# Sums of weights for block products: VectorE additions, or ScalarE copies with accumulating GpSimd transfers

## The chip, the core and the metric

The kernel runs on one core of one Trainium2 chip. A core has five engines that each work through their own queue in order: TensorE (PE in the profile, with its weight loads as PEld), VectorE (DVE), ScalarE (ACT), GpSimd (POOL) and SyncE (SP). SP only issues transfers here; the transfers of all queues run on 16 DMA engines. The metric is the device time of one execution in microseconds.

## The reference

Two parts follow one another. The first is an attention with a decaying state, for 4 batches, 8 heads, 768 tokens and 48 channels per head:

```python
for t in range(S):
    cur = einsum('bhd,bhe->bhde', u * k_t, v_t)
    y[:, :, t] = einsum('bhd,bhde->bhe', r_t, state + cur)
    state = w_t[..., None] * state + einsum('bhd,bhe->bhde', k_t, v_t)
```

Its output, laid out as 3072 tokens by 384 channels, is the input `x` of the second part. Its weights are `w_in` (384 by 2048) and `w_out` (2048 by 384), given in 64-bit floating point:

```python
h = x @ w_in
g = h * clip(h + 3.0, 0.0, 6.0) / 6.0
out = g @ w_out
```

## The kernel before

**Tiling.** The tokens are cut into 24 chunks of 128, and four chunks form a block; there are six blocks. Attention runs chunk by chunk: two scans over the decay on DVE (`back_scan` L372, `fore_scan` L381), products that make K (`make_k` L392) and R (`make_r` L396), score products on PE (L440), a masked copy of them on DVE (`above` L447), a transposition of K (L456) whose result ACT copies (`turned_k`, "kn", L461), diagonal terms on ACT (`diagonal` L431), products that read the state (L514) and the values (L523), products that write the state (`write` L536), and state updates on DVE or POOL (L469, L477, L485). For the first seven chunks `early(i)` puts K and R on DVE, from chunk 7 on it puts them on POOL. `own_dot` (L415) multiplies r, u and k on PE for the first nine chunks. In block 0, `read_last`, `leave_last` (L576), `read_rest` (L584) and `leave_rest` (L594, L596) bring a chunk's output into the block's `xT`.

**The weights** come as 64-bit words in 16 loads of 768 KB into the tile `bits` (three buffers). ACT (`low_scaled` L340, `low_whole` L344) and DVE (`high_shift` L349, `high_join` L354, `high_low` L359) turn each load into 32-bit numbers, by way of the tiles `more` and `top`.

**The products.** Block 0 computes its up products plainly (`up` L639, with `ramp` L629 on ACT and `gate` L650 on DVE behind each), and so its down products for chunks 0 and 1 (`down` L658, `drain` L665). All else is done in 2 by 2 blocks with seven products instead of eight (`up_product` L740, `down_product` L791). This form needs sums of quarters of the operands. The sums of activations are made for every block (`sum_x` L722, `sum_g` L776). The sums of weights are made once, when the last weight is converted: `sum_in` (L700) makes three sums of quarters of `w_in` in the freed buffers `top` and `more` and overwrites one quarter in place, in 16 additions of 128x256. `sum_out` (L712) makes three sums of quarters of `w_out` in the freed `bits` and overwrites one quarter in place, in eight additions of 128x768. The products read the sums; `up_read` (L749 on ACT, L751 on DVE) and `down_read` (L804 on ACT, L806 on DVE) join the seven results.

**The order.** A class `Plan` sets each engine's order. Every step is added with its engine, an assumed duration, the steps it needs, a key, and the rings of buffers it holds. `order()` places the steps one by one: on the engine that can start first, the ready step with the smallest key. Keys are due times, shifted by constants at the top of the file (`LAG`, `AHEAD`, `LEAD`, `START`, `CONV`, `UP`, `SUMS`, `OWN`). The instructions are then issued in that order, and each engine runs its own in order. In the opening, up to the first `up`, `emit` also fills gaps that the plan sees on PE with `spin` matmuls of the identity (L1130), whose results nobody reads:

```python
if engine == "PE" and spinning:
    for _ in range(int(self.FILL * (self.start[n] - last) / self.SPIN)):
        self.spin()
```

The functions that the change touches, and what calls them:

Of the kernel before, what the change touches and what calls it, by code (L numbers as in the profile page):

```python
# [8 lines left out]
F32 = mybir.dt.float32  # L9
# [17 lines left out]

LAG = 6.1
AHEAD = -3.5
LEAD = 2.5  # L30
BEHIND = (-1, -1, -1, 0, 6, 7)
BY_PE = 9
OWN = 0.07
SOLO = (0, 2, 3, 4, 5)
EARLY = 7
START = (-118.3, -135.2, -24.4, -60.3, -5.9, 13.2)
CONV = (-100.6, 7.2)
UP = (-68.7, 1.2, -9.3, 6.3)
SUMS = (52.1, 1.4)
LEAST = 2.0 ** -60  # L40
# [42 lines left out]
class Plan:  # L83
# [20 lines left out]
    def add(self, name, engine, us, emit, after=(), key=0.0, hold=(), port=False, kb=0.0, lands=0.0,  # L104
            dmas=1):

        assert name not in self.steps, name
        self.steps[name] = (engine, us, emit, tuple(after), key, tuple(hold), port, kb, lands, dmas)

    def order(self):  # L110
# [13 lines left out]
        while open_:  # L124
            best = {}
            for n in open_:
                engine, us, _, after, key, hold, shared, kb, _, dmas = steps[n]
                t = free.get(engine, 0.0)
                if kb and len(lanes) + dmas > self.LANES:
                    t = max(t, lanes[len(lanes) + dmas - self.LANES - 1])  # L130
                for a in after:
                    if steps[a][0] != engine:
                        t = max(t, end[a] + self.HOP)
                for r, _ in hold:
                    over = len(held[r]) - self.rings[r]
                    if over >= 0:
                        ends = sorted(max(end[a] + (self.HOP if steps[a][0] != engine else 0.0) for a in frees)
                                      for frees in held[r] if all(a in end for a in frees))
                        if len(ends) <= over:
                            t = None  # L140
                            break
                        t = max(t, ends[over])
                if t is None:
                    continue
                if shared:
                    t = max(t, port)
                best.setdefault(engine, []).append((t, key, n))
            assert best, sorted(open_)
            t, engine = min((min(c)[0], e) for e, c in best.items())
            _, _, n = min((key, t_, n) for t_, key, n in best[engine] if t_ <= t + 1e-9)  # L150
            _, us, _, _, _, hold, shared, kb, lands, dmas = steps[n]
            start[n] = t
            free[engine] = end[n] = t + us
            if kb:
# [3 lines left out]
                end[n] = max(done + self.LAND, lands)  # L158
                lanes += [end[n]] * dmas
            if shared:  # L160
                port = t + us
# [26 lines left out]
def fast_path(tc, feat, tok, wflat, ub, ug, moe_w_in, moe_w_out, out, flag, n_chunks):  # L188
# [21 lines left out]
    with ExitStack() as ctx:  # L210
# [475 lines left out]

        def sum_in(s, q):

            at = (s - 1 if s < 3 else 2) * HF + q
            if s != 3 and at // 6 not in a_sums:  # L690
                name = ("top", "more")[at // 6 % 2]
                a_sums[at // 6] = wk.tile([128, 6 * 128], F32, name=name)
            (a11, a21), (a12, a22) = ([w_in[:, q:q + 2, j, y, :] for y in range(2)] for j in range(2))
            def sums(k):
                at = k * HF + q
                return a_sums[at // 6][:, at % 6 * 128:(at % 6 + 2) * 128].rearrange("p (q j) -> p q j", q=2)
            out_, in0, in1, op = {1: lambda: (sums(0), a21, a22, ALU.add), 2: lambda: (sums(1), sums(0), a11, ALU.subtract),
                                  3: lambda: (a21, a11, a21, ALU.subtract),
                                  4: lambda: (sums(2), a12, sums(1), ALU.subtract)}[s]()
            nc.vector.tensor_tensor(out=out_, in0=in0, in1=in1, op=op)  # L700

        def sum_out(t, x):

            m, h = HF // 2, DM // 2
            if t != 3 and x == 0:
                b_sums[t] = io.tile([128, HF, h], F32, name="bits", bufs=3)
            (b11, b12), (b21, b22) = ([w_out[:, k * HF + x * m:k * HF + (x + 1) * m, y * h:(y + 1) * h] for y in range(2)]
                                      for k in range(2))
            T = {k: v[:, x * m:(x + 1) * m, :] for k, v in b_sums.items()}
            out_, in0, in1 = {1: lambda: (T[1], b12, b11), 2: lambda: (T[2], b22, T[1]), 3: lambda: (b12, b22, b12),  # L710
                              4: lambda: (T[4], b21, T[2])}[t]()
            nc.vector.tensor_tensor(out=out_, in0=in0, in1=in1, op=ALU.subtract)  # L712

        def sum_x(bk, part):
# [4 lines left out]
            (b11, b12), (b21, b22), (c1, c2) = ([b["xT"][:, j, y * HB:(y + 1) * HB] for y in range(2)] for j in range(NCC))  # L719
            for o, x, y in (((T[:, 0], b12, b11), (T[:, 1], b22, T[:, 0])),  # L720
                            ((b12, b22, b12), (T[:, 2], b21, T[:, 1]), (T[:, 3], c1, c2)))[part]:
                nc.vector.tensor_tensor(out=o, in0=x, in1=y, op=ALU.subtract)  # L722

# [19 lines left out]
        def up_read(bk, q, what):  # L743
# [3 lines left out]
            src = b["p", q, {"s1": "A", "u": "A", "c21": "A", "c22": "A", "c11": "B", "v": "C", "c12": "C"}[what]][:, :HB]  # L747
            if what in ("s1", "u", "v", "c21"):
                nc.scalar.copy(out=to, in_=src)  # L749
            else:  # L750
                nc.vector.tensor_add(to, src, to)  # L751

# [8 lines left out]
        def sum_g(bk, p, k, x):  # L761
# [7 lines left out]
            def part(h, c):  # L769
                if bk == 0:  # L770
                    return b["g", h][:, x * m:(x + 1) * m, (2 * p + c) * L:(2 * p + c + 1) * L]
                return b["g", p][:, h * HF + x * m:h * HF + (x + 1) * m, c * L:(c + 1) * L]
            (a11, a21), (a12, a22) = ([part(h, c) for c in range(2)] for h in range(2))
            o, x0, x1, op = {1: (S, a21, a22, ALU.add), 2: (S, S, a11, ALU.subtract), 3: (a21, a11, a21, ALU.subtract),
                             4: (S, a12, S, ALU.subtract)}[k]
            nc.vector.tensor_tensor(out=o, in0=x0, in1=x1, op=op)  # L776
# [17 lines left out]
        def down_read(bk, p, what):  # L794
            b = blocks[bk]
            h = DM // 2
            if what == "s1":
# [3 lines left out]
                  "v": o[:, 1, h:], "c22": o[:, 1, h:]}[what]  # L801
            src = b["d", p, {"s1": "A", "u": "A", "c21": "A", "c22": "A", "c11": "B", "v": "C", "c12": "C"}[what]][:, :h]
            if what in ("s1", "u", "v", "c21"):
                nc.scalar.mul(to, src, 1.0 / 6.0)  # L804
            else:
                nc.vector.scalar_tensor_tensor(out=to, in0=src, scalar=1.0 / 6.0, in1=to, op0=ALU.mult, op1=ALU.add)  # L806

# [59 lines left out]
        def do(fn, *args):  # L867
            return lambda: fn(*args)
# [154 lines left out]

        for n_, (s_, q) in enumerate((s_, q) for s_ in (1, 2, 4, 3) for q in range(0, HF, 2)):
            at = ({1: 0, 2: 1, 4: 2}.get(s_, 9)) * HF + q
            hold = []
            if s_ != 3 and at % 6 == 0:
                hold = [(("top", "more")[at // 6 % 2], ["end"])]
            before = [f"sin{x}.{q}" for x in ({2: (1,), 4: (2,)}.get(s_, ()))] + [f"sin{s_}.{q - 2}"] * (q > 0)
            if s_ == 3:  # L1030
                before += all_up + [f"sin1.{q}"]
            if s_ == 1 and q == 0:
                before += [f"{ready}{len(pairs) - 1}"]
            if s_ in (2, 4) and q == 0:
                before += [f"sin{s_ // 2}.{HF - 2}"]
            plan.add(f"sin{s_}.{q}", "DVE", 0.36, do(sum_in, s_, q), before, SUMS[0] + n_ * SUMS[1] / 4, hold, port=True)
        for n_, (t_, x) in enumerate((t_, x) for t_ in (1, 2, 4, 3) for x in range(2)):
            before = [f"sout{y}.{x}" for y in ({2: (1,), 4: (2,)}.get(t_, ()))] + [f"sout{t_}.0"] * x
            if t_ == 3:
                before += [f"down0.{c}.{HF - 1}" for c in classic] + [f"sout1.{x}"]  # L1040
            if t_ == 1 and x == 0:
                before += [f"{ready}{len(pairs) - 1}"]
            plan.add(f"sout{t_}.{x}", "DVE", 0.95, do(sum_out, t_, x), before, SUMS[0] + 4 * SUMS[1] + n_ * SUMS[1] / 2,
                     [("bits", ["end"])] * (t_ != 3 and x == 0), port=True)
        sin = [f"sin{s_}.{HF - 2}" for s_ in range(1, 5)]
        sout = [f"sout{t_}.1" for t_ in range(1, 5)]

        for bk in range(NB):
# [34 lines left out]
            for p in range(bk == 0, 2):  # L1083
# [14 lines left out]
                for n_, (k_, after, hold) in enumerate((  # L1098
                        (1, [], [("bankA", [r + "c21"])]), (2, [], [("bankB", [r + "c11"])]), (5, [], [("bankC", [r + "c12"])]),
                        (6, [r + "s1"], []), (3, [r + "v"], []), (7, [r + "u"], []), (4, [r + "c22"], []))):  # L1100
                    for x in range(2):
                        before = gated(0, NFC) if k_ != 1 else gated(4 * x, 4 * x + 4)
                        if k_ in (5, 6, 7, 3):
                            before = [g_ + f"{ {5: 1, 6: 2, 7: 3, 3: 4}[k_] }.{x}"]
                        chain = {6: 1, 7: 6, 4: 7, 3: 5}.get(k_)
                        plan.add(d_ + f"{k_}.{x}", "PE", 1.3, do(down_product, bk, p, k_, x),
                                 before + [d_ + f"{k_}.0"] * x + [d_ + f"{chain}.1"] * bool(chain) + after + [f"sout{t_}.{x}" for t_ in ({5: 1, 6: 2, 7: 3, 4: 4}.get(k_),) if t_], at + 2.6 * n_ + 1.3 * x + (2.6 if k_ == 4 else 0), hold if x == 0 else ())
                for what, eng, after, key in (("s1", "ACT", [d_ + "1.1"], 1), ("v", "ACT", [d_ + "5.1"], 3), ("u", "ACT", [d_ + "6.1"], 4),
# [361 lines left out]
```

## Time and profile before

| | value |
|---|---|
| median of 3 runs (lowest to highest) | 573.67 us (573.64 to 573.75) |
| span of the profiled execution, first to last instruction | 570.5 us |
| its own time beside the span | not recorded apart; the median of the runs lies 3.2 us above the span |
| mean granted TensorE clock | 0.992 |
| busy: PE, PEld, DVE, ACT, POOL | 558.8, 501.8, 405.2, 273.5, 100.3 us |
| DVE sums of weights, 16 of L700 and 8 of L712 | 7.5 and 8.5 us, between 102 and 133 us |
| first product of `up` | 32.3 us |

Times in the profile count from the first instruction. A matmul of 32-bit numbers shows as two records. PE's busy time is modelled from its queue, so a busy PE isn't PE at its peak, and filler counts as busy. Granted clock is the share of full speed that the array was given. A wait is put down to the engine that came last.

### The profile page before, as it was taken

How to read it: one execution, taken by the hardware profiler on the slowest of the kernel's cores; microseconds unless marked ns; L12 is line 12 of the kernel's file. 1: busy time of each engine (PE TensorE's matmuls, PEld its weight loads, DVE VectorE, ACT ScalarE, POOL GpSimd, SP SyncE). 2: the span in 40 equal slices, each digit the busy share in tenths (PEclk: the TensorE clock that was granted, in tenths of full speed). 3: DMA queues.
4: the chain of work that ended last, by engine and by line, in shares of the span. 5: the costliest groups of instructions: out<-in, count | busy, mean ns of one | idle time of the engine just before them, and what ended most of it. 6: DMA issues, size and time to landing. Idle time of an engine off the chain costs nothing.

```text
span 570.5 us, 13575 instructions
## 1 busy us (share of the span) xinstructions
PE 558.8 (98%) x5636; PEld 501.8 (88%) x5636; DVE 405.2 (71%) x713; ACT 273.5 (48%) x724; POOL 100.3 (18%) x111
## 2 busy tenths in 40 slices
PE   8999899999999999999999999999999999999996
PEld 8898587689888999988999988999988999988996
DVE  7989989988687858767879767879656625255350
ACT  4778664642565633276633366633266611355100
POOL 2000000245513321223123133123122000000000
PEclk9989899999999999999999999999999999999999
DMA  8977822531613236830368360366100001000001
GB/s 279 310 237 223 275 66 63 158 111 42 182 56 90 87 124 204 241 100 9 125 206 274 98 167 7 128 199 225 41 16 2 9 1 36 29 1 1 1 15 47
DMA packets 23078, 63.98 MB, mean 112 GB/s; under 512 B 3120, under 2 KB 10352, under 8 KB 23008
## 3 DMA queue, kind: packets, MB, share of 16 engines
q1 hardware_dynamic: 22880, 63.02, 36.0%
q8 instruction: 46, 0.75, 0.6%
q14 instruction: 24, 0.20, 0.1%
q10 hardware_dynamic: 128, 0.00, 0.0%
HBM read 57.31 MB, written 4.72 MB: 109 GB/s over the span
## 4 chain that ended last, share of the span: by engine, by line
PE 94%; DVE 2%; DMA 1%; ACT 1%; issue 1%; SPq 0%; DVEq 0%; ACTq 0%
PE bankA L791 20%; PE bankA L740 18%; PE bankC L791 10%; PE bankC L740 9%; PE bankB L740 6%; PE bankB L791 5%; PE bankC L639 3%; PE bankA L639 3%; PE bankA L658 3%; PE y_ps L514 3%; PE y_ps L523 2%; PE y_ps L536 2%; PE ps L456 2%; PE bankB L440 2%; DMA feat_in<-in_feat_dram 1%; PE bankA L1130 1%
## 5 line engine op out<-in xcount | busy, mean ns | idle before, releaser
L749 ACT COPY g<-bankA 128x256 f32<-128x256 f32 x120 | 44.3, 371 | 58.7 <-PE bankA L740 56.6
L791 PE MATMUL bankA<-w_out,g 128*128 128x192 f32 x352 | 63.9, 328 | 0.0
L629 ACT ACTIVATE clip<-g,three 128x512 f32<-128x512 f32 x80 | 57.9, 723 | 7.9 <-DVE g L751 7.2
L740 PE MATMUL bankA<-xT,w_in 128*128 128x256 f32 x240 | 60.2, 383 | 0.0
L791 PEld LDWEIGHTS bankA<-w_out,g 128*128 128x128 f32 x352 | 57.9, 190 | 0.9
L759 DVE SCALAR_TENSOR_TENSOR g<-clip,g 128x512 f32<-128x512 f32 x80 | 56.4, 707 | 2.8 <-ACT clip L629 2.6
L804 ACT ACTIVATE o<-bankA 128x192 f32<-128x192 f32 x33 | 10.9, 330 | 88.8 <-PE bankA L791 88.8
L740 PEld LDWEIGHTS bankA<-xT,w_in 128*128 128x128 f32 x240 | 44.8, 190 | 6.0
L431 ACT ACTIVATE A<-eyes,dg 128x64 f32<-128x64 f32 x192 | 49.2, 336 | 0.4
L606 ACT COPY xT<-y_ps 48x256 f32<-48x256 f32 x80 | 29.3, 366 | 37.3 <-PE y_ps L523 36.4
L392 POOL TENSOR_TENSOR K<-feat_in,E 112x512 f32<-112x512 f32 x17 | 21.5, 1266 | 136.6 <-PE bankC L440 121.6
L740 PE MATMUL bankB<-xT,w_in 128*128 128x256 f32 x160 | 41.1, 379 | 0.0
L751 DVE TENSOR_TENSOR g<-bankB,g 128x256 f32<-128x256 f32 x40 | 16.9, 423 | 32.4 <-PE bankB L740 30.7
L396 POOL TENSOR_TENSOR W<-feat_in,W 112x512 f32<-112x512 f32 x17 | 23.1, 1356 | 87.2 <-DVE W L381 87.2
L751 DVE TENSOR_TENSOR g<-bankC,g 128x256 f32<-128x256 f32 x40 | 16.8, 421 | 28.3 <-PE bankC L740 28.2
L740 PEld LDWEIGHTS bankB<-xT,w_in 128*128 128x128 f32 x160 | 30.4, 190 | 4.1
L381 DVE TENSOR_TENSOR_SCAN W<-feat_in,start 112x520 f32<-112x520 f32 x24 | 30.6, 1274 | 3.1 <-PE y_ps L514 3.0
L372 DVE TENSOR_TENSOR_SCAN E<-feat_in,back 112x520 f32<-112x520 f32 x24 | 30.0, 1250 | 2.5 <-DMA feat_in<-in_feat_dram 2.4
L791 PE MATMUL bankA<-bits,g 128*128 128x192 f32 x176 | 30.3, 328 | 0.4 <-DVE o L806 0.4
L791 PE MATMUL bankB<-w_out,g 128*128 128x192 f32 x176 | 30.4, 326 | 0.0
L791 PEld LDWEIGHTS bankA<-bits,g 128*128 128x128 f32 x176 | 28.8, 190 | 0.9 <-DVE o L806 0.7
L791 PEld LDWEIGHTS bankB<-w_out,g 128*128 128x128 f32 x176 | 28.9, 190 | 0.0
(277 smaller groups left out, 1213.8 us busy)
## 6 DMA issues: line engine op xcount, KB each, us to landing
feat_in<-in_feat_dram SPq DMA_DIRECT2D x23, 675.9 KB, 5.6
bits<-in_moe_w_in_dram SPq DMA_DIRECT2D x8, 768.0 KB, 9.6
bits<-in_moe_w_out_dram SPq DMA_DIRECT2D x8, 768.0 KB, 4.7
feat_in<-in_moe_w_in_dram SPq DMA_DIRECT2D x8, 768.0 KB, 4.3
feat_in<-in_moe_w_out_dram SPq DMA_DIRECT2D x8, 768.0 KB, 4.2
rk_in<-in_tok_dram SPq DMA_DIRECT2D x15, 384.0 KB, 5.9
v_in<-in_tok_dram SPq DMA_DIRECT2D x24, 192.0 KB, 4.0
out_dram<-o SPq DMA_DIRECT2D x24, 192.0 KB, 2.1
```

The lines of the kernel that those rows point to most:

```text
L372: nc.vector.tensor_tensor_scan(out=E_[:, ::-1], data0=d["w"][:, :0:-1], data1=back.rearrange("q p t -> q (p t)")[:, ::-1], initial=0.0, op ...
L381: nc.vector.tensor_tensor_scan(out=W_, data0=d["w"][:, :-1], data1=starts[i % 2].rearrange("q p t -> q (p t)"), initial=0.0, op0=ALU.mult, ...
L396: early(i).tensor_mul(d["R"], d["r"], d["R"])
L431: nc.scalar.activation(out=d["A"][:, h, :], in_=eyes, func=ACT.Copy, scale=d["dg"][:, h])
L606: nc.scalar.copy(out=blocks[bk]["xT"][g * GP:g * GP + D, :, at:at + HL], in_=st[i]["y_ps"][(g ^ a) * GP:(g ^ a) * GP + D, a, :, :])
L629: nc.scalar.activation(out=c[:, :m], in_=src, func=ACT.Relu, bias=three, scale=1.0)
L639: nc.tensor.matmul(h_ps[:, :(c1 - c0) * L], lhsT=w_in[:, f // 2, j, f % 2, :], rhs=b["xT"][:, j, c0 * L:c1 * L], start=(j == 0), stop=(j = ...
L740: nc.tensor.matmul(b["p", q, to][:, :HB], lhsT=w, rhs=rhs, start=(n == 0 and k in (1, 2, 5)), stop=(n == len(terms) - 1 and k in (2, 3, 4) ...
L749: nc.scalar.copy(out=to, in_=src)
L751: nc.vector.tensor_add(to, src, to)
L759: nc.vector.scalar_tensor_tensor(out=g, in0=b["r", q, p], scalar=6.0, in1=g, op0=ALU.min, op1=ALU.mult)
L791: nc.tensor.matmul(b["d", p, to][:, :h], lhsT=a, rhs=w(), start=(f == 0 and k in (1, 2, 5)), stop=(f == HF - 1 and k in (2, 3, 4)), skip_g ...
```

## The change

The sums of weights leave VectorE. For each sum ScalarE first copies one quarter into the new tile (`begin_out`, `begin_in`), and then a transfer issued by GpSimd adds the other quarter to it on the way (`accum_op=ALU.add`). The second sum of a chain adds the first, the third adds the second, so each of these transfers waits until the one before has landed. The two quarters that are overwritten get their addition by a transfer alone. There are 13 transfers: four for `w_out`, nine for `w_in`, because tiles of `top` and `more` hold six of eight pieces.

A transfer can add[...], so signs move: ScalarE negates one quarter of `w_in` (`negate`), the sums of activations change their signs (two of five in `sum_x` become `scalar_tensor_tensor`), and reading the products multiplies by -1 or subtracts where it copied or added.

The constants of the order are set anew, with larger `LAG`, `AHEAD` and `LEAD`. `Plan.add` takes one more value, `late`, by which the end of a step lies behind its engine's time; the transfers are given `SUM_LATE`. The order of the other work, and the number of `spin` matmuls (53 before, 43 after), change with the constants.

```diff
-LAG = 6.1
-AHEAD = -3.5
-LEAD = 2.5
+LAG = 9.862
+AHEAD = -7.975
+LEAD = 4.9
-OWN = 0.07
+OWN = -0.92
-START = (-118.3, -135.2, -24.4, -60.3, -5.9, 13.2)
-CONV = (-100.6, 7.2)
-UP = (-68.7, 1.2, -9.3, 6.3)
-SUMS = (52.1, 1.4)
+START = (-110.18, -114.56, -39.57, -55.4, 7.53, 6.26)
+CONV = (-105.26, 7.89)
+UP = (-83.83, 3.17, -14.31, 3.08)
+SUMS = (-15.47, 158.38)
+SUM_LATE = 8.0
...
-            nc.vector.tensor_tensor(out=out_, in0=in0, in1=in1, op=op)
...
+        def begin_in(k):
+            for at in range(k * HF // 6, (k * HF + HF - 1) // 6 + 1):
+                if at not in a_sums:
+                    a_sums[at] = wk.tile([128, 6 * 128], F32, name=("top", "more")[at % 2])
+            src = unit(*((0, 1), (0, 0), (1, 0))[k])
+            for q, n, to in parts_of(k):
+                nc.scalar.copy(out=to, in_=src[:, q:q + n])
+        def sum_in(k):
+            if k == 3:
+                nc.gpsimd.dma_start(out=unit(0, 1), in_=unit(0, 0), accum_op=ALU.add)
+                return
+            if k == 0:
+                for q, n, to in parts_of(0):
+                    nc.gpsimd.dma_start(out=to, in_=unit(1, 1)[:, q:q + n], accum_op=ALU.add)
+                return
...
+                nc.gpsimd.dma_start(out=cut(k), in_=cut(k - 1), accum_op=ALU.add)
+        def negate():
+            nc.scalar.mul(unit(2, 1), unit(2, 1), -1.0)
+        def begin_out(t):
+            b_sums[t] = io.tile([128, HF, DM // 2], F32, name="bits", bufs=3)
+            nc.scalar.copy(out=b_sums[t], in_=quarter(*{1: (0, 1), 2: (1, 1), 4: (1, 0)}[t]))
+        def sum_out(t):
+            to, src = {1: lambda: (b_sums[1], quarter(0, 0)), 2: lambda: (b_sums[2], b_sums[1]),
+                       4: lambda: (b_sums[4], b_sums[2]), 3: lambda: (quarter(0, 1), quarter(1, 1))}[t]()
+            nc.gpsimd.dma_start(out=to, in_=src, accum_op=ALU.add)
...
-            for o, x, y in (((T[:, 0], b12, b11), (T[:, 1], b22, T[:, 0])),
-                            ((b12, b22, b12), (T[:, 2], b21, T[:, 1]), (T[:, 3], c1, c2)))[part]:
-                nc.vector.tensor_tensor(out=o, in0=x, in1=y, op=ALU.subtract)
+            for o, x, y in (((T[:, 0], b11, b12), (T[:, 1], T[:, 0], b22)),
+                            ((b12, b22, b12), (T[:, 2], T[:, 1], b21), (T[:, 3], c1, c2)))[part]:
+                if x.tensor is y.tensor:
+                    nc.vector.tensor_tensor(out=o, in0=x, in1=y, op=ALU.subtract)
+                else:
+                    nc.vector.scalar_tensor_tensor(out=o, in0=x, scalar=-1.0, in1=y, op0=ALU.mult, op1=ALU.subtract)
...
-            if what in ("s1", "u", "v", "c21"):
+            if what in ("s1", "u"):
                 nc.scalar.copy(out=to, in_=src)
+            elif what in ("v", "c21"):
+                nc.scalar.mul(to, src, -1.0)
             else:
-                nc.vector.tensor_add(to, src, to)
+                nc.vector.tensor_tensor(out=to, in0=to, in1=src, op=ALU.subtract if what == "c22" else ALU.add)
```

In `sum_g` two of the four operations exchange addition and subtraction, and in `down_read` the factor 1/6 takes a minus sign for two of the seven results. In the plan the DVE steps `sin` and `sout` give way to ACT steps `bin`, `bout` and `negate`, which wait for the last conversion or the last `up`, and to POOL steps `sin` and `sout`:

```diff
+        for n_, t_ in enumerate((1, 2, 4, 3)):
+            before = [f"bout{t_}"] if t_ != 3 else [f"down0.{c}.{HF - 1}" for c in classic] + ["bout1"]
+            before += [f"sout{t_ // 2}"] * (t_ in (2, 4))
+            plan.add(f"sout{t_}", "POOL", 1.2, do(sum_out, t_), before, SUMS[0] + n_ * 3, late=SUM_LATE)
...
+        for k_ in range(4):
+            before = [f"bin{k_}"] + [f"sin{k_ - 1}"] * (k_ > 0) if k_ < 3 else all_up + ["bin0"]
+            plan.add(f"sin{k_}", "POOL", 1.2 * (1, 2, 2, 1)[k_], do(sum_in, k_), before, SUMS[1] + k_ * 3, late=SUM_LATE)
+        plan.add("negate", "ACT", 1.03, negate, all_up, SUMS[1] + 9)
```

## The prediction, made before the changed kernel ran

> **What bounds the kernel now.** I read the busy shares first, then the busy time by stretches, then the chain that ended last in the opening, then the waits of PE.
>
> ```profile
> PE 558.8 (98%) x5636; PEld 501.8 (88%) x5636; DVE 405.2 (71%) x713; ACT 273.5 (48%) x724; POOL 100.3 (18%) x111
> ```
>
> PE is the bound. Where does it still lose time? Columns: length, busy us of PE, PEld, DVE, ACT, POOL (with instruction counts), granted clock, DMA share, GB/s.
>
> ```profile
> 0.00:32.30 32.30, 30.22 (x390) 27.86 (x391) 28.78 (x49) 20.21 (x52) 4.03 (x15) 0.95 0.93 284
> 32.30:60.00 27.70, 27.30 (x185) 22.48 (x184) 24.57 (x43) 23.16 (x47) 0.00 (x0) 1.00 0.77 240
> 60.00:90.00 30.00, 28.34 (x360) 21.41 (x359) 27.26 (x49) 16.41 (x39) 0.00 (x0) 0.94 0.42 133
> 90.00:120.00 30.00, 29.06 (x430) 21.52 (x429) 27.34 (x51) 15.99 (x53) 5.56 (x4) 1.00 0.44 127
> 120.00:152.00 32.00, 30.88 (x495) 28.20 (x486) 26.35 (x44) 12.98 (x41) 16.85 (x15) 1.00 0.33 97
> 152.00:526.00 374.00, 373.78 (x3562) 341.73 (x3562) 256.70 (x458) 179.16 (x482) 73.84 (x77) 1.00 0.32 97
> ```
>
> After 152 us PE has no gap; only the first 152 us can give anything back. From the first up product (32.3) to 152, PE idles 0.40 + 1.66 + 0.94 + 1.12 = 4.1 us. Before 32.3 its "busy" is largely filler, the `spin` matmuls of L1130, as the chain in the opening shows (start, us, what):
>
> ```profile
> 17.70 0.32 PE y_ps L514 x4
> ...
> 18.44 0.96 PE bankA L1130 x6
> ...
> 22.32 2.28 PE bankA L1130 x16
> ...
> 25.27 0.42 PE bankA L1130 x2
> ...
> 29.94 2.54 PE bankA L1130 x12
> 32.48 0.65 PE bankC L639 x3
> ```
>
> Filler stands on the path: the first up product needs chunk 1's `leave` (the ACT copies L594/L596, done at 30.28), but PE works off 12 filler records until 32.5. Eight at 22.3 likewise end 0.6 us after the S they wait for (L469, done at 23.95). The remaining waits of PE:
>
> ```profile
> PE y_ps L536 <- ACT kn L461: 1.6, 2, 0.9
> PE bankA L1130 <- POOL ident masks.py:199: 1.4, 1, 1.4
> PE y_ps L584 <- ACT xT L576: 0.6, 1, 0.6
> PE bankB L440 <- DVE A L447: 0.5, 1, 0.5
> PE bankA L791 <- DVE o L806: 0.4, 1, 0.4
> PE bankA L658 <- DVE w_out L359: 0.4, 1, 0.4
> ```
>
> None is a wait for a sum of weights. These sums, the 16 of L700 (7.5 us) and 8 of L712 (8.5 us), run on DVE between 102 and 133, beside a PE that hardly waits. So the 16 us taken from DVE are not 16 us of time.
>
> **What the Trainium skill says.** "DMA: Bandwidth & Descriptors", § SWDGE vs HWDGE vs iDMA: an accumulating transfer can only be issued by GpSimd, whose cores write the descriptors; § Anatomy of one DMA prices a GpSimd copy at 2.0 us + bytes/436e3. This trace has no such transfer; its nearest are 768 KB loads issued by SP, landing in 4.2 to 4.7 us. "SBUF — State Buffer", § Who interferes with whom: a DVE instruction with two SBUF inputs blocks GpSimd reads, and the reverse. The trace agrees: L392 on POOL takes 1184 ns in the median and 2575 at 114.8, beside L712; L712 itself 950 and 1948. "TensorE: Matmul & The Clock Gate", Part 1: the array falls to half rate after a window of some 3.4 us with little activity. The trace agrees: clock 0.52 from 29.7 to 32.4, where a filler pair costs 0.42 us against 0.29 at full clock; again 0.50 near 68.
>
> **The change, part by part.**
>
> *1. Opening (keys).* By instruction order. On DVE two conversion steps (L349 0.55 + L354 0.96) move behind chunk 0's L469, and chunk 2's scan (L372 1.24 + L376) moves behind chunk 1's. ACT takes its first conversion after chunk 1's `diagonal`, not before. Filler between chunk 0's first read and the first up product goes from 3 + 8 + 1 + 6 = 18 matmuls to 5 + 6 + 1 + 2 = 14. Worked along the chain:
> - L469 of chunk 0 ended at 17.65 with the 1.5 us ahead of it; now 16.4. First read: 17.70 becomes 16.5.
> - Its filler grows by two (2 x 0.3): the rest of chunk 0 starts at about 18.8 (19.4), ends at 21.8 (22.3).
> - Six filler (1.7) instead of eight: 23.6; chunk 1's L469 now follows its kvs copy at once (22.8), so it doesn't hold. First read of chunk 1 at 23.6 (24.6).
> - Then dot and rest as before, to 28.0; one dot (0.9) replaces one transpose (0.9); two filler at 0.3 to 0.45 each. `leave` of chunk 1 ends at 29.1 behind eight L431 (2.0). First up product at **29.5 instead of 32.4: -2.9 us** (-1 to -3.5).
>
> *2. Can DVE feed the earlier start?* In DVE's order 15.8 us of work lie between the first gate and the eighth w_in conversion; adding waits for clips, that conversion ends at about 48.8, and PE asks at 48.7. Next, score 3 waits for L447 of chunk 2 (about 0.9), and the rest of chunk 2 for its copy (0.7); w_out conversions 2 to 5 end at 59.4, 61.8, 64.1, 66.4, about when PE asks. That is 1.8 us of stall against the 1.6 listed now, with no reserve: **+0.8** (0 to 3).
>
> *3. DVE sums out.* -16.0 us of DVE from 102 to 133. Worth nothing directly. But PE's order spreads out there: eight products (2.6 us) stand between the transposes L456 and L536 where none did at 150.2 (wait 0.68), and attention work stands before the last product at 145.5 (wait 0.45). **-1.1** (0 to -1.6).
>
> *4. ACT copies.* Three of 128x1536, six pieces of 128x256 to 768, one negation of 128x1024. From L340 (0.92 at 768), L629 (0.72 at 512) and L749 (0.37 at 256): 3 x 1.7 + 4.0 + 1.2 = 10.3 us. ACT is busy 16.0 of 30 and 13.0 of 32 there, so it fits; the danger is order. The three long ones stand in a row (5.1 us at about 88); queued behind are chunk 5's kvs copy and a clip. In PE's order the up product that needs that clip's bank is over 8 us later: **0** (to +2 if that cover goes).
>
> *5. POOL transfers.* Thirteen, 5.1 MB read. POOL keeps its order, so K and R of chunks 7 and 8 (L392, L396) stand behind transfers that wait for earlier ones to land. With landing time D and 1.3 us per issue (unknown: SP's is 0.4, POOL's longest row 2.6; I take its 128x512 mean), starting at the last conversion (about 86; now 85.1) plus the first copy: 90.2 + 5 issues and pieces (6.4) + 2D, then R7 and K8. PE wants them at about 122. D: 3.8 by the page's price, 4.7 by the nearest row; with the destination read too, up to twice that. I take 8 (4 to 20): POOL is free at 113, 9 us early. The last sums wait for the last classic down (about 121): 121 + 1.3 + 3.9 + 8 = 134, wanted by the first L740 at 146. **0**; break-even D about 12. The DMA share there is 0.33 to 0.44, so loads have room.
>
> *6. Signs.* No instruction more on DVE: two T sums per block become scalar_tensor_tensor (128x256: L650 0.41, L722 0.42); ACT's `mul` for `copy` is nearest L804 (0.33 for 192). SP issues nothing new. **0** (-0.5 to +1, over the 374 us without slack).
>
> Sum: 570.5 - 2.9 + 0.8 - 1.1 = 567.3 us. The profiled span, 570.5, lies 3.2 below the median 573.67; with the same around it, **570.5 us**. A measurement of this kernel can tell about 0.2% (1.15 us) from no change.
>
> **Rivals.**
> - *A. The early start is eaten by DVE.* DVE is 24.6 of 27.7 and 27.3 of 30 busy from 32 to 90; a late conversion stops PE at once (L658 <- L359, 0.4). Then step 2 costs 3 instead of 0.8 and step 3 gives little: 573. Against: DVE gets ahead by some us as well. Chance 0.14.
> - *B. Slower: POOL's queue.* If D is 16 us (descriptor writing, contention with DVE's two-input reads), each us beyond 12 counts twice before R7 and K8: +8, so 578. It decides from D of about 13.5, where the loss equals the gain. For it: no row bounds D, POOL rows stretch twofold. Against: nearest landing 4.7. Chance 0.20.
> - *C. Half clock falls on real work.* A low window at 29 to 32 now meets up products instead of filler: +1.7, so 572. Chance 0.10.
> - *D. More is recovered:* stalls of 60 to 152 go as well, 568. Chance 0.06.
> - The forecast: 0.50.
>
> **Numbers.** Faster: forecast, D, and most of C, 0.64; same: most of A, some of C, 0.14; slower: B and the rest of A, 0.22. The range: down to 567.3 (3.5 in step 1, 1.6 in step 3, no stall in step 2: 570.5 - 0.6 - 0.5 - 0.8 = 568.6, and D below it), up to 577.5, nearly B. Faster alone spans 567.3 to 572.5.
>
> **What would show it.** Step 1: first L639 at 29 to 30.5, 43 filler matmuls. Step 2: PE waits for L359 and L447 under 2.5 us before 75. Step 3: no L700/L712 rows on DVE, fewer waits for kn. Step 5: landing of the POOL transfers under 12, and no PE wait for W or K after 110. The prediction is wrong if the first L639 stays past 31.5, or if PE idles several us between 110 and 150 behind POOL or DMA.

## The result, and the profile after

The changed kernel is slower: 577.42 us in the median of 20 executions against 573.2 for the kernel before (20 executions), ratio 1.0081 (95% interval 1.0058 to 1.0105), about **+4.6 us**. Executions more than 1.5% above the fastest of their kernel are left out of the ratios and clocks of this document. The profiled execution took 577.96 us with a span of 575.9. Executions of one kernel spread over some 7 us, and most of that goes with the clock that the array was granted: the changed kernel's lie between 574.84 us at a mean clock of 0.993 and 582.41 us at 0.979. So each kernel below has its mean clock beside its ratio.

The page after, its busy times and its DMA queues (packets, MB, share of 16 engines' span):

```profile
PE 559.4 (97%) x5618; PEld 500.7 (87%) x5618; DVE 393.2 (68%) x689; ACT 283.1 (49%) x734; POOL 114.3 (20%) x124
...
q1 hardware_dynamic: 22880, 63.02, 35.8%
q0 software_dynamic: 5328, 5.24, 6.1%
```

DVE lost 12 us (the 16 of the sums went, its other rows together grew by 4), and PE's own work stayed the same. The second queue is new: 5.24 MB in 5328 packets. The same stretches as before (length, busy us of PE, PEld, DVE, ACT, POOL, granted clock, DMA share, GB/s):

```profile
0.00:32.30 32.30, 28.84 (x380) 26.26 (x381) 26.66 (x44) 18.95 (x53) 3.01 (x15) 0.95 0.92 264
32.30:60.00 27.70, 25.36 (x242) 21.21 (x240) 25.08 (x47) 22.98 (x45) 0.00 (x0) 1.00 0.82 252
60.00:90.00 30.00, 28.92 (x235) 22.31 (x229) 25.10 (x40) 17.85 (x42) 0.00 (x0) 0.83 0.36 120
90.00:120.00 30.00, 28.70 (x370) 21.43 (x368) 24.02 (x47) 20.72 (x51) 11.90 (x11) 1.00 0.88 171
120.00:152.00 32.00, 30.45 (x515) 26.70 (x516) 16.49 (x28) 15.26 (x49) 17.88 (x19) 1.00 1.04 225
152.00:526.00 374.00, 372.83 (x3630) 339.67 (x3629) 257.65 (x455) 178.76 (x476) 81.56 (x81) 1.00 0.32 99
```

The account of the span, after against before: first up product at 31.6 instead of 32.3 (-0.7); PE idle from 32.3 to 152 is 2.34 + 1.08 + 1.30 + 1.55 = 6.3 instead of 4.1 (+2.2); the clock from 60 to 90 is 0.83 instead of 0.94, 30 x 0.11 = +3.3; idle from 152 to 526 is 1.17 instead of 0.22 (+0.95). That is +5.7 for a span 5.4 longer. The DMA share at 120 to 152 is 1.04, where it was 0.33.

PE's waits in the changed kernel, up to 60 and from 60 to 160 us (total, times, longest):

```profile
...
PE ps L458 <- ACT kn L463: 1.3, 1, 1.3
PE ps L458 <- DVE K L394: 1.2, 1, 1.2
PE bankB L442 <- DVE A L449: 0.6, 1, 0.6
PE y_ps L516 <- ACT kvs L545: 0.5, 1, 0.5
...
PE y_ps L538 <- DMA v_in<-in_tok_dram: 2.9, 2, 1.6
...
```

The last is new in kind: PE waits for a load. The chain of waits shows both times (start, us, what):

```profile
109.60 10.54 DMA v_in<-in_tok_dram
120.14 0.14 issue
120.28 0.62 PE y_ps L538 x24
...
121.44 9.37 DMA v_in<-in_tok_dram
130.81 0.14 issue
```

A 192 KB load of `v_in`, 4.0 us in the median before (2.5 for those issued between 80 and 160 us), takes 10.5 and 9.4 us here. It can start only when a buffer comes free, at 109.5, and PE wants it at 118.7. With 4 us it would have been in time by 5 us. What it shares the DMA engines with are the accumulating transfers (issued by POOL; KB, us to landing, between 80 and 160 us):

```profile
q0 software_dynamic: 5328, 5.24, 44.2%
q1 hardware_dynamic: 3168, 8.48, 35.6%
...
bits<-bits POOLq DMA_DIRECT2D x2, 768.0 KB, 13.1
...
more<-top POOLq DMA_DIRECT2D x2, 256.0 KB, 14.9
```

They move 5.24 MB to the other queue's 8.48, but take more of the engines' time.

### The profile page after: what moved, and what is told of

The parts are those of the page before. It is cut to its first block, busy times and chain, and to the rows that moved or that the text cites. A ratio compares the mean times of both kernels' runs of the same rounds, so it can differ in the third digit from the quotient of the medians.

```text
span 575.9 us, 13566 instructions
## 1 busy us (share of the span) xinstructions
PE 559.4 (97%) x5618; PEld 500.7 (87%) x5618; DVE 393.2 (68%) x689; ACT 283.1 (49%) x734; POOL 114.3 (20%) x124
## 3 DMA queue, kind: packets, MB, share of 16 engines
q0 software_dynamic: 5328, 5.24, 6.1%
## 4 chain that ended last, share of the span: by engine, by line
PE 91%; DMA 5%; DVE 2%; issue 1%; ACT 0%; SPq 0%; DVEq 0%; ACTq 0%
PE bankA L827 20%; PE bankA L774 18%; PE bankC L827 10%; PE bankC L774 9%; PE bankB L774 6%; PE bankB L827 5%; PE bankC L641 4%; PE bankA L641 3%; DMA v_in<-in_tok_dram 3%; PE y_ps L516 2%; PE bankA L660 2%; PE y_ps L525 2%; PE y_ps L538 2%; PE ps L458 2%; PE bankB L442 1%; DMA feat_in<-in_feat_dram 1%
## 5 line engine op out<-in xcount | busy, mean ns | idle before, releaser
L795 DVE SCALAR_TENSOR_TENSOR g<-clip,g 128x512 f32<-128x512 f32 x80 | 57.6, 726 | 7.4 <-ACT clip L631 7.4
L774 PE MATMUL bankA<-xT,w_in 128*128 128x256 f32 x240 | 62.1, 382 | 0.0
L774 PEld LDWEIGHTS bankA<-xT,w_in 128*128 128x128 f32 x240 | 44.5, 190 | 5.8
L841 ACT ACTIVATE o<-bankA 128x192 f32<-128x192 f32 x33 | 10.9, 330 | 66.5 <-PE bankA L827 66.2
L783 ACT COPY g<-bankA 128x256 f32<-128x256 f32 x80 | 29.8, 372 | 26.9 <-PE bankA L774 25.0
L774 PE MATMUL bankB<-xT,w_in 128*128 128x256 f32 x160 | 41.1, 379 | 0.0
L787 DVE TENSOR_TENSOR g<-g,bankC 128x256 f32<-128x256 f32 x40 | 16.8, 419 | 27.6 <-PE bankC L774 25.9
L398 POOL TENSOR_TENSOR W<-feat_in,W 112x512 f32<-112x512 f32 x17 | 25.1, 1479 | 45.2 <-DVE W L383 45.2
L774 PEld LDWEIGHTS bankB<-xT,w_in 128*128 128x128 f32 x160 | 30.4, 190 | 4.1
L787 DVE TENSOR_TENSOR g<-g,bankB 128x256 f32<-128x256 f32 x40 | 16.7, 417 | 23.6 <-PE bankB L774 19.0
L394 POOL TENSOR_TENSOR K<-feat_in,E 112x512 f32<-112x512 f32 x17 | 20.2, 1188 | 53.7 <-PE bankC L442 41.8
```

What stands on the lines that cost most here:

```text
L398: early(i).tensor_mul(d["R"], d["r"], d["R"])
L774: nc.tensor.matmul(b["p", q, to][:, :HB], lhsT=w, rhs=rhs, start=(n == 0 and k in (1, 2, 5)), stop=(n == len(terms) - 1 and k in (2, 3, 4) ...
L787: nc.vector.tensor_tensor(out=to, in0=to, in1=src, op=ALU.subtract if what == "c22" else ALU.add)
L795: nc.vector.scalar_tensor_tensor(out=g, in0=b["r", q, p], scalar=6.0, in1=g, op0=ALU.min, op1=ALU.mult)
```

## The experiments

The first theory after this trace: two losses, one by the constants (the opening, and a "thin" stage, in which PE has little work, with half clock behind it), one by the transfers' traffic. The rivals: all by the constants; all by the sums; GpSimd's queue instead of traffic. "At equal clock" is the distance to the kernel before in us at a clock of 0.992, from one common slope for all executions here, with an offset for each kernel (about 300: 0.47 us for each 0.001 of clock, scatter 0.7 us). It is a rough aid: it treats half clock on filler like half clock on work.

| kernel | ratio to before (95%) | mean clock | at equal clock |
|---|---|---|---|
| before | 1 | 0.9911 | 0 |
| the change | 1.0081 (1.0058 to 1.0105) | 0.9877 | +2.9 |
| e1 sums alone | 1.0064 (1.0036 to 1.0091) | 0.9911 | +3.5 |
| e2 constants alone | 1.0230 (1.0194 to 1.0267) | 0.9757 | +5.7 |
| e3 no transfers | 1.0020 (0.9996 to 1.0045) | 0.9868 | -0.8 |
| e4 OWN back | 1.0147 (1.0116 to 1.0177) | 0.9907 | +8.0 |
| e5 small transfers | 1.0023 (1.0002 to 1.0043) | 0.9872 | -0.3 |
| e6 plain transfers | 1.0029 (1.0009 to 1.0048) | 0.9863 | -0.2 |
| e7 change, filler in the thin stage | 1.0080 (1.0055 to 1.0104) | 0.9918 | +5.6 |
| e8 before, filler in the thin stage | 1.0018 (0.9998 to 1.0037) | 0.9938 | +2.6 |
| e9 old constants, no transfers | 1.0029 (1.0011 to 1.0048) | 0.9924 | +2.0 |
| e10 sums on GpSimd | 1.0342 (1.0312 to 1.0373) | 0.9812 | +14.0 |
| e11 before, less filler | 1.0081 (1.0052 to 1.0110) | 0.9790 | -2.3 |
| e12 change, more filler | 1.0117 (1.0076 to 1.0159) | 0.9877 | +5.2 |
| e13 before, more filler | 1.0076 (1.0046 to 1.0105) | 0.9902 | +3.9 |

**The halves of the change.** e1 undoes the seven constants of the opening and of the attention's lead, e2 does them alone. `SUMS`, which places the sums, stays new in e1 and old in e2.

```diff
 # e1: the changed kernel; e2 is the reverse edit on the kernel before
-LAG = 9.862
+LAG = 6.1
 ... (and AHEAD, LEAD, OWN, START, CONV, UP)
```

> The changed kernel with the seven constants of the opening and of the attention's lead (LAG, AHEAD, LEAD, OWN, START, CONV, UP) set back to the values of before; copies, transfers and signs stay. Theory (two losses: about 2 us by the new constants in the opening and at 50 to 75 us, about 3 us by the transfers, which hold up loads of v_in): the transfers' part alone, +1 to +3 us against before, with v_in loads landing in 8 us or more while transfers run, and the first up product back near 32.4. Rival 1 (all by the constants): within 1 us of before. Rival 2 (all by the sums): +4.6 us, as the whole change.

> The kernel before with only the seven new constants; the sums stay on VectorE with their old keys. Theory of two losses: +1.5 to +2.5 us against before, with PE idle 2 us or more between 48 and 62 us, a half-clock stretch behind it, and no PE wait for v_in after 100. Rival 1 (all by the constants): +4.6 us. Rival 2 (all by the sums): within 1 us of before.

e1 came at +3.7 us, a little over what two losses gave it, but not by their mechanism: `v_in` lands in 6.9 us in the median, and its PE waits for no load. The first up product is at 33.5. e2 came at +13.2, which nobody expected. Up to 90 us its trace is the changed kernel's (PE busy 12.67 of 15 at 45 to 60, clock 0.66 at 60 to 75). Then DVE's sums, which e2 keeps, stand from 109 to 129 ahead of scans that the new constants want early. POOL's timeline and then PE's show it (start, us, instruction, idle before and what ended it):

```profile
136.94 1.61 POOL L396 TENSOR_TENSOR W<-feat_in,W 112x512 f32<-112x512 f32 x1 [10.29 <-DVE W L381]
```

```profile
156.40 1.10 PE L514 MATMUL y_ps<-W,S 48*48 48x64 f32 x32 [5.32 <-POOL S L469]
```

POOL waits 10.3 us for the scan, chunk work falls behind, PE stops for 5.3 us, and half clock follows from 154 to 165. So 13.2 and 3.7 alone make 4.6 together: under the new constants the sums on DVE, at their old keys, are in the way, and the parts don't add. Whether new keys for these sums would have mended e2 was not tested.

**The transfers: queue or traffic.** e3 leaves them out; e5 cuts each to 8 of 128 partitions; e6 keeps all bytes but copies instead of accumulating.

```diff
 # e3: return at the head of sum_in, no dma_start in sum_out
 # e5:
-nc.gpsimd.dma_start(out=to, in_=src, accum_op=ALU.add)
+nc.gpsimd.dma_start(out=to[:8], in_=src[:8], accum_op=ALU.add)
 # e6:
+nc.gpsimd.dma_start(out=to, in_=src)
 # the same in the three lines of sum_in
```

> The changed kernel with the 13 accumulating transfers left out (their additions are not done; ScalarE's copies stay, and the plan keeps the steps with their times). Theory of two losses: 2.9 us faster than the changed kernel, so +1.5 to +2 against before; v_in loads land in about 4 us and PE waits for none. Rival 1 (constants): as the changed kernel, +4.6. Rival 2 (sums): within 1 us of before.

> The changed kernel with each of the 13 accumulating transfers cut to 8 of its 128 partitions (the rest of the sums is left out); order, chain of waits and issues on GpSimd's queue stay. Theory (the transfers cost by their traffic, which holds up loads): as without transfers, +1.2 to +2 us against before, v_in loads landing in 2.5 to 4 us, no PE wait for v_in. Rival (GpSimd's queue: issues and waits of the chain hold K and R back): still some 2 to 3.5 us above the kernel without transfers, so +4 or more, with PE or DVE waiting for K, W or S from GpSimd.

> The changed kernel with the same 13 transfers as plain copies, without the accumulation (the sums are then not made); order and issues are the same. Theory (accumulating makes the transfers long, since the destination is read too): they land in about half the time of the 9.5 to 16.7 us seen in the changed kernel, the DMA share between 105 and 135 falls from over 1.0 to 0.7 or so, and the time is 1.5 to 3 us below the changed kernel. Rival (their many packets of about 1 KB and the sharing with loads make them long, accumulation or not): landing within 20% of the changed kernel's, same time to 1 us.

All three come at 1.2 to 1.7 us above before, with intervals below the change's, so the accumulating transfers cost **3.0 to 3.5 us** (each of these differences is known to about 2 us either way). None has a PE wait for `v_in` after 100 us. The traces agree. From 105 to 120 and from 120 to 135, before, then the change, then e6 (columns as above):

```profile
105.00:120.00 15.00, 15.00 (x210) 10.48 (x209) 13.34 (x21) 6.36 (x20) 4.37 (x3) 1.00 0.38 115
120.00:135.00 15.00, 15.00 (x187) 13.80 (x178) 14.44 (x23) 6.30 (x20) 7.39 (x6) 1.00 0.30 88
```

```profile
105.00:120.00 15.00, 13.70 (x209) 9.73 (x207) 11.28 (x21) 9.56 (x27) 9.28 (x10) 1.00 1.05 196
120.00:135.00 15.00, 13.45 (x267) 10.60 (x268) 5.34 (x9) 7.37 (x24) 12.94 (x13) 1.00 1.16 229
```

```profile
105.00:120.00 15.00, 15.00 (x220) 11.21 (x218) 12.98 (x23) 10.66 (x30) 6.40 (x10) 1.00 0.86 265
120.00:135.00 15.00, 15.00 (x277) 11.85 (x276) 5.33 (x9) 8.67 (x29) 11.55 (x13) 1.00 0.92 278
```

PE idles 2.9 of these 30 us in the change and not at all in the other two. In e5 all 13 issues and the order of POOL's queue are those of the change, and `v_in` lands in 3.2 us. So the issues as such cost nothing that these runs can tell. But in e5 and e6 the chain of transfers is shorter too (each lands in 3.8 to 5.6 and in 3.3 to 7.4 us), and in the change POOL's queue stood close behind the load. Its lines, then PE's:

```profile
118.76 0.86 POOL L743 DMA_DIRECT2D bits<-bits  x1 [3.21 <-DMA bits<-bits]
119.33 1.49 POOL L398 TENSOR_TENSOR W<-feat_in,W 112x512 f32<-112x512 f32 x1
```

```profile
120.28 0.62 PE L538 MATMUL y_ps<-v_in,kn 64*64 64x48 f32 x30 [1.58 <-DMA v_in<-in_tok_dram]
...
121.13 0.27 PE L442 MATMUL bankB<-W,K 48*64 48x64 f32 x1
```

POOL waits 3.2 us for a transfer to land, and so R of chunk 7 (L398) is done only at 120.8. PE uses it at 121.1, 1.6 us late because of `v_in`. With the load in time PE would have wanted R at about 119.5 and stood still some 1.3 us for POOL instead (an estimate from these lines; in e5 R is done at 119.3, just before PE takes it at 119.4). So the harm comes from the transfers' length. The wait that ends last is the load's; what POOL's queue alone would cost is not separated from it. e6 moves the same bytes without harm:

```profile
q0 software_dynamic: 1328, 5.24, 19.8%
...
bits<-bits POOLq DMA_DIRECT2D x2, 768.0 KB, 6.3
...
v_in<-in_tok_dram SPq DMA_DIRECT2D x5, 192.0 KB, 2.6
...
more<-top POOLq DMA_DIRECT2D x2, 256.0 KB, 6.6
```

Against the change's lines above: a quarter of the packets, 19.8% of the engines' time instead of 44.2%, landing in half the time. The theory of e6 holds in the landing time, about half, and in the time, 3 us below the change; its DMA share fell less than expected, to 0.86 and 0.92 instead of 0.7. That plain copies have four times larger packets was in neither theory, and whether the size or the accumulation makes the transfers long is not separated.

e9 asks what DVE's relief is worth under the old constants:

```diff
 # the changed kernel with e1's constants and e3's missing transfers
```

> The changed kernel with the seven constants of before (as in the run of the sums alone) and also without the 13 transfers (their additions are not done). It shows what DVE's relief is worth under the old constants. Theory (transfers cost 3 to 4 us by their traffic under either set of constants; taking 16 us from DVE is worth 1 us at most): 3 to 3.5 us below the run of the sums alone, so -0.5 to +0.5 against before, clock 0.991. Rival (under the old constants the loss came from the copies on ACT or from the other signs): still +2 or more.

It came at +1.7, 1.2 us above the theory's range and just below the rival's. Compared with e1, the transfers cost 2.0 us here; the intervals overlap, so under the old constants their price is likely but not firm, and as e1's PE waits for no load, its path is open. And with DVE free of 16 us of sums the time is no shorter. Why it loses 1.7 stays open, and the rival, ACT's copies or the other signs, is not excluded: PE's new waits there are L417 with 1.4 in the opening, which was a late one in this profile, and L774 for ACT's L783 with 1.0.

**OWN.** One constant put the product of r and k ahead of chunk 1's decay scan on DVE:

```profile
9.92 0.69 DVE L407 TENSOR_TENSOR rk<-feat_in 112x512 f32<-112x512 f32 x1 [1.50 <-PE ps L458]
10.53 1.23 DVE L374 TENSOR_TENSOR_SCAN E<-feat_in,back 112x520 f32<-112x520 f32 x1
```

```profile
14.01 0.58 PE L458 MATMUL ps<-ident,K 112*128 112x112 f32 x4 [1.24 <-DVE K L394]
```

```diff
-OWN = -0.92
+OWN = 0.07
```

> The changed kernel with OWN alone set back to 0.07, which puts chunk 1's decay scan ahead of its product of r and k on DVE again. Theory: the scan starts 0.6 us sooner, PE's wait of 1.24 us for K near 14 shrinks to 0.6 and no half-clock stretch follows it, so the first read comes 1 to 1.5 us sooner and the first up product at 30.5 to 31.5; time 0.5 to 1.5 us below the changed kernel. Rival (the late landing of the decay load alone made the opening late): same opening to 0.3 us, same time.

The first read came 1.0 us sooner (17.95 instead of 18.98) and PE's wait for K went, as the theory said. The rest was wrong: the order then has 53 filler matmuls as before and not 44, the first up product is at 33.5, and the order after 100 us is another one, with PE waits of 2.4 for A, 1.9 for `v_in` and 1.3 for a sum of activations (`sum_g`). The time is 3.8 us above the change. A constant of this planner can't be judged by the place it is named for.

**The clock: filler in the thin stage.** e7 and e8 let `emit` fill the plan's gaps at 49 to 68 us as well, e7 with 15 more matmuls and e8 with 8 more (e8 leaves out `turn3`).

```diff
-            if engine == "PE" and spinning:
+            if engine == "PE" and (spinning or n in ("turn3", "score3", "first2", "read2", "first3", "read3")):
 ... (and `spinning` ends as it did before)
```

> The changed kernel with filler matmuls also in the gaps that the plan sees on PE at 49 to 66 us (ahead of turn3, score3, first2, read2, first3 and read3: 16 more). Theory (thin PE work at 57 to 62 us brings half-clock windows that then fall on down products): mean granted clock 0.991 or more against 0.9877, time 1 to 2 us below the changed kernel, +2.5 to +3.5 against before. Rival (the windows do not come from that stage): clock as in the changed kernel, time the same or up to 1 us longer, since filler stands ahead of work.

> The kernel before with filler matmuls also in the gaps of the plan ahead of score3, first2, read2, first3 and read3 (8 more, at 58 to 68 us). Theory: the half-clock window at 66 to 70 us goes, 1 to 1.7 us faster than before, clock 0.994. Rival: same clock, same time or up to 1 us longer.

Stretches of 2 us, the changed kernel first, then e7 (columns as above):

```profile
58.00:60.00 2.00, 1.00 (x42) 0.74 (x40) 1.86 (x5) 0.48 (x1) 0.00 (x0) 1.00 0.71 223
60.00:62.00 2.00, 1.25 (x23) 1.03 (x16) 1.97 (x6) 0.52 (x2) 0.00 (x0) 1.00 0.19 33
...
66.00:68.00 2.00, 1.90 (x11) 0.59 (x9) 1.84 (x3) 1.34 (x2) 0.00 (x0) 0.50 0.90 275
```

```profile
58.00:60.00 2.00, 2.00 (x68) 1.32 (x66) 1.59 (x5) 1.95 (x3) 0.00 (x0) 1.00 1.06 313
60.00:62.00 2.00, 1.83 (x18) 1.19 (x10) 1.75 (x5) 0.48 (x1) 0.00 (x0) 1.00 0.52 141
...
66.00:68.00 2.00, 1.89 (x56) 1.60 (x56) 1.97 (x3) 0.15 (x2) 0.00 (x0) 1.00 0.19 77
```

In the change PE is 2.25 of 4 us busy at 58 to 62, and from 62 to 73 it runs at half clock, on down products (2.86 us for what takes 1.29 at 55.7). With filler there this stretch is at full clock, and the mean clock over the executions rises from 0.988 to 0.992, in the kernel before from 0.991 to 0.994. So the thin stage is what brings these windows. But the time is the same in e7, and in e8 it is 1 us longer, with an interval that still includes no change at all: the filler stands ahead of work and costs what the clock gives. Both theories were right on the clock and wrong on the time.

**The clock: filler in the opening.** e11 takes filler away from the kernel before, e13 and e12 add it.

```diff
-int(self.FILL * (self.start[n] - last) / self.SPIN)
+int((self.FILL if last == self.COLD else 0.5) * (self.start[n] - last) / self.SPIN)   # e11; 1.0 in e12 and e13
```

> The kernel before with less filler in the opening: 39 matmuls instead of 53, the first 15 kept. It tests the premise of step 1, that filler stands on the path. Premise: first read and first up product come earlier, 1 to 2.5 us faster than before, same clock. Rival (filler holds the clock up, and what it takes it gives back): mean granted clock down to 0.988 or less, first up product within 1 us of before, time +0 to +2 us.

> The changed kernel with more filler in the opening: 55 matmuls instead of 44 (the first 15 kept), about the 53 of before. Theory (the new constants take filler away, and the granted clock falls for it): mean granted clock back from 0.988 to 0.990 to 0.991, the transfers' cost stays (PE waits for v_in 2 to 3 us), time the same as the changed kernel to 1 us, since what the clock gives the filler takes. Rival (the clock under the new constants is low for another reason, the thin stage at 57 to 62 us alone): clock stays at 0.988, time 1.5 to 3 us longer.

> The kernel before with more filler in the opening: 67 matmuls instead of 53. With the run of less filler it gives three points. Theory (clock against filler, an optimum near what is there): clock 0.993 or more, time +0.5 to +2.5 us. Rival (more filler still pays): 0.5 to 1.5 us faster than before.

For the kernel before with 39, 53 and 67 filler matmuls: +4.6, 0 and +4.4 us. With 39 the clock falls to 0.979, as the rival said, but the time is longer than it gave. The premise of e11 failed: its first read (18.89 instead of 17.70) and its first up product (33.64 instead of 32.32) come later, with the decay load taken up at 10.07 instead of 8.88. That it would be 2.3 us faster at equal clock is only the rough line's figure. With 67 the clock is nearly the same (0.990, where the theory had 0.993 or more) and the filler is plain cost, above the theory's 2.5: the first up product moves to 36.46. So added filler does stand on the path, but filler taken out here gave nothing back. In e12 the clock of the change doesn't move (0.9877) and the time is about 2 us longer, with overlapping intervals, as its rival said. So the missing filler is not why the change's clock is low; the thin stage at 57 to 62 is what remains, and e7 shows it directly.

**Another engine for the sums.** e10 issues before's 24 additions on GpSimd.

```diff
-            nc.vector.tensor_tensor(out=out_, in0=in0, in1=in1, op=op)
+            nc.gpsimd.tensor_tensor(out=out_, in0=in0, in1=in1, op=op)
 # the same in sum_out; in the plan both are steps of POOL, with 0.65 and 1.9 us
```

> The kernel before with its 24 additions issued on GpSimd instead of VectorE (same tiles, signs and keys; in the plan 0.65 and 1.9 us each): no copies, no transfers. From L392 (1.18 us for 512 elements) 16 x 0.6 + 8 x 1.8 = 24 us of GpSimd between 90 and 135. Theory: DVE's relief costs no traffic this way, so -1 to 0 us against before. Rival (GpSimd's queue and the shared reads with VectorE hold K and R of chunks 7 and 8 back): +2 us or more, with PE or DVE waiting for K or W from GpSimd.

+19.6 us, as the rival said in kind, though not by a late K or W but, as far as the trace shows, where GpSimd and DVE read at the same time. One DVE addition (L776, 0.69 us as a rule) takes 7.88, and POOL's timeline shows beside what:

```profile
125.37 7.88 DVE L776 TENSOR_TENSOR S__1534<-S__1534,g 128x512 f32<-128x512 f32 x1 [0.58 <-PE bankC L791]
```

```profile
126.01 5.33 POOL L712 TENSOR_TENSOR bits<-w_out,bits 128x768 f32<-128x768 f32 x3
131.30 2.54 POOL L700 TENSOR_TENSOR w_in<-w_in 128x256 f32<-128x256 f32 x3
```

Six additions stand back to back on POOL from 126.0 to 133.8, and DVE's ends at 133.25, near their end. PE stops 6.5 us for its result. No version here beats the kernel before.

## Why the prediction was wrong, step by step

- *What bounds the kernel*: right. PE's work is the same (559.4 against 558.8), and the differences are idle time or clock, all but about 1 us of them in the first 152 us.
- *Step 1 (-2.9): mis-sized, -0.7 in the profile.* From the first read to the first up product it gave 13.0 us; 12.7 were measured. The part ahead failed: 16.5 predicted, 18.98 measured. The step took the landing of chunk 1's decay load from one trace. In the traces DVE begins on it between 8.9 and 10.9 us, under either set of constants. In the change it began at 9.92, OWN put 0.6 us ahead of the scan, PE was idle for 1.24, and half clock from 14 to 19 made 14 filler records 2.72 us long. Where the load came at 8.94 (e7), the first read was at 16.75. Over the profiles with the opening's filler untouched, the first up product is at 31.0 to 34.0 with the new constants (mean of six 32.0) and at 32.2 to 35.4 with the old ones (mean of five 33.2): -1.2. The filler matmuls are 44 (88 records), not 43.
- *Step 2 (+0.8): mis-sized, above all by the 3.3 us of clock.* Its own figures, 1.8 against 1.6, give only +0.2; it wrote +0.8 for want of a reserve. PE's idle time from 32.3 to 90 grew by 1.4 us. The waits listed at 49 to 62 are 3.0 us against its 1.8, for kn, A, kvs and xT and not for conversions. Its price was missed: the half-clock stretch behind it, 5.1 us lost at 60 to 90 instead of 1.8. Rival C had this mechanism, but at 29 to 32 and with 1.7 us.
- *Step 3 (-1.1): right, and more than eaten by step 5.* From 90 to 152 PE idled 2.06 us before (0.94 + 1.12). In e3, e5 and e6 it is busy for 62.00 of 62 us, so these kernels get 2.1 us back there. In the change the transfers take 2.9 in the same stretch. The gain needs the new constants: in e9 PE still idles 1.5 us there.
- *Steps 4 and 6 (0): not refuted, but not shown.* PE waits for no copy by name. But after 152 us it idles 1.17 us in the change, and 1.2 in e3, e5 and e6, where it had 0.22; the waits listed are for DVE, L812 with 0.6 and L843 with 0.4. All these kernels have the copies, the signs and the new constants, so the 0.95 us more may belong to any of them; step 6 allowed up to +1. e9 leaves the same question open.
- *Step 5 (0): the step that failed most.* D was 6.2 to 16.9 us, mostly 12.5 to 15.7, instead of 8, and so above the step's own break-even; the first transfer was issued at 97.35 instead of 90.2. The step looked for harm in POOL's queue and dismissed the DMA engines with "the DMA share there is 0.33 to 0.44, so loads have room". For D it went by 768 KB loads with 4.2 to 4.7 us, but the same page has eight more of them, in the opening, where the DMA share is 0.93:

```profile
bits<-in_moe_w_in_dram SPq DMA_DIRECT2D x8, 768.0 KB, 9.6
```

It allowed for a read of the destination in the landing time and not in the engines' time. The transfers took 44% of all 16 engines over 80 us, and the loads that are issued just in time came late, with POOL's queue close behind: +3.0 to +3.5. (The plan is blind in the same place: `sin` and `sout` are added without `kb`, so its link carries no byte of them.)
- *Rival B* had the right sign and nearly the time (578), from a place that was not the last: PE's waits name neither K nor W from POOL. But it was no idle rival, since R of chunk 7 would have held PE for some 1.3 us had `v_in` come in time.
- *The sum*: -3.2 predicted, +4.6 measured. The transfers are 3.0 to 3.5 of it; without them the new constants and copies are still 1.2 to 1.7 above before, their small gain at equal clock (0.2 to 0.8, within what that aid can tell) undone by a lower clock (0.986 to 0.987 against 0.991). That the time came near rival B's and not near the forecast's is the sum of several misses, and not one term. Of the 3.2 us added to the span 1.7 lie outside it; by the rest the profiled execution was quicker than the median.

## What to carry to other kernels

Before adding transfers, add up the DMA engines' time and not the bytes, and look for loads that are issued just in time: here they were what the busy DMA delayed first, and the queue that waits for its own transfers came next. Where the array's clock follows its activity, filler and thin stretches have a price on both sides, and filler taken out is no gain until the clock is seen. Constants of an order belong to one distribution of work: with the sums back on DVE at their old keys the new ones cost 13 us.

## What the runs showed of the hardware

- Accumulating transfers between SBUF tiles took 2.2 times the DMA engines' time of plain ones with the same bytes, beside the same loads (44.2% against 19.8% of 80 us), in four times the packets (5328 against 1328, so 0.98 KB and 3.9 KB each), and their issue on GpSimd took 1.55 to 2.21 us against 0.54 to 0.56 (L727).
- Half clock comes in stretches whose loss is a multiple of 1.71 us (1.71, 3.41, 5.12 summed from windows of 1 us, the end of the span left out), so of 3.4 us each at a clock of 0.50. How many there are changes between executions of one kernel (mean clock 0.979 to 0.993 for the change). Where they fall differs too: the change and e5 have the same opening, and the first stretch is at 14 to 19 us in one and at 28 to 36 in the other. Low activity without a long gap was enough: PE was busy for 2.25 us of 58 to 62, with no single gap over 0.7 us, ahead of the half clock from 62 to 73. The Trainium skill, "TensorE: Matmul & The Clock Gate", Part 1, states such a window, which runs freely, of about 3.4 us; the traces agree.
- The Trainium skill, "SBUF — State Buffer", § Who interferes with whom, says that a DVE instruction with two SBUF inputs and GpSimd's reads block each other. The trace of e10 agrees and gives a size: with six GpSimd additions back to back, one DVE addition of 0.69 us took 7.88.
